# Attention and a gated MLP on one core: another order of the same tasks, and other engines for some of them

## The chip, the cores and the metric

The kernel runs on one core of one Trainium2 chip. The metric is the device time of one execution in microseconds; the median of three runs before the change is 718.39 us (718.02 to 721.24).

## The reference

Eight batches, eight heads, 576 positions, head size 64, model width 512. The reference computes, for every batch and head, scores with a bias that depends on the two positions through a small network, a softmax, and the product with v; the eight heads of a position are then put side by side, and the result goes through a convolution of five taps with a sigmoid (the gate) and two projections.

```python
scores = scale * q @ k.T
x = log1p(abs(i - j)) / log1p(max(i, 1))
bias = relu(x * w1 + b1) @ w2              # one value per head, i and j
attn = softmax(scores + bias)
x = attn @ v                               # heads side by side: 8 x 576 x 512
gate = sigmoid(sum(conv_w[k] * xp[:, k:k+576] for k in range(5)))
out = (gate * (x @ w_val)) @ w_out
```

## The kernel before, in words

The whole work is cut into 3338 tasks, each a function that issues a few instructions on one engine or one DMA. A task lists the tasks it depends on, the engines that may run it with a cost for each, and the buffers it takes and uses. In this version nothing is scheduled when the program is built: two tables, `ORDER` (line 49) and `WHERE`, say in which order the tasks are issued and on which engine each stands (V is DVE, A is ACT, G is POOL, P is TensorE, S is the DMA queue of SP). `Plan.order` walks through the tables, checks that what a task depends on stands before it, and hands out buffers: a ring is a first-in, first-out list of slots, and a slot goes back to the list when the last user of its buffer has been listed. The order of the tables therefore fixes three things: the order of the instructions on each engine, the order of the DMAs in SP's queue, and which earlier tile each buffer is taken over from. Every engine works its list strictly in order.

The stages, with the names and lines that the prediction uses:

- The bias table, 36 strips of 16 positions. Per strip four relu tasks (L450 on ACT, L452 on DVE or POOL), one matmul task (L478), one eviction (L492 on ACT, L494 on DVE), one store to a table in DRAM (L503). Eight strips make one block of 128 rows, of which each bias load (L528, for the last 64 rows L532) reads two heads; a load depends on all stores of its block.
- Attention, 32 pairs of heads, each in five row blocks. Per block: the scores (L929, L949), on DVE the sum with the bias and the row maximum (L800), on ACT the exponential with the row sum (L813, L819), on DVE the reciprocal (L822), on POOL the normalisation (L826), on DVE a transposition in 32x32 blocks (L973, L975). The first six pairs transpose on TensorE instead (L858 to L891) and evict with ACT or DVE (L360, L362). When all five blocks of a pair are turned, TensorE multiplies with v in three tasks of 96 short matmuls each (L1030; the AV tasks), and the result is scaled out of PSUM (L368, L370).
- The weights of the two projections arrive as 64-bit numbers, which DVE and POOL take apart in some ten steps per piece (L548 to L582, L373, L707, L364).
- The MLP, per batch: the convolution (first tap L1095 or L1097; products L1103 on ACT or L1105 on POOL, added up by L1108 on POOL; one of four channel groups adds on DVE with L1093), the sigmoid (L1125), the splitting of x into two halves of 16 bits (L360, L362, L364, then the rest L373), the first projection (L1170), the gate (L1180), the splitting of the gated values, the second projection (L1233), the scaling out of PSUM (L368, L370) and the store.

PSUM holds four tiles for all matmul tasks together (`sp=4`), so a score task can start only when an earlier tile has been read out. Biggest shares of the work are fixed to an engine: L800 and the transpositions to DVE, L813 to ACT, L826 and L1108 to POOL. Free to move are evictions, scalings, splits, the products L1103/L1105 and the relus.

Of the kernel before, what the change touches and what calls it, by code (L numbers as in the profile page):

```python
# [49 lines left out]
    21, 22, 24, 23, 25, 14, 17, 606, 0, 16, 15, 35, 18, 1, 2, 38, 26, 37, 7, 3, 4, 36, 379, 261, 39, 9, 8, 10, 28,  # L50
    29, 11, 42, 44, 377, 30, 31, 5, 32, 257, 119, 40, 121, 378, 375, 45, 267, 268, 122, 120, 258, 43, 123, 56, 33,
    46, 49, 253, 58, 19, 255, 256, 254, 59, 57, 60, 124, 27, 50, 41, 51, 12, 263, 52, 53, 63, 259, 20, 65, 64, 66,
    67, 70, 385, 91, 262, 264, 34, 47, 73, 72, 71, 74, 92, 54, 84, 6, 94, 93, 95, 86, 87, 85, 68, 88, 265, 48, 77,
    61, 78, 125, 80, 266, 386, 79, 98, 99, 376, 100, 81, 112, 427, 89, 105, 101, 82, 115, 113, 13, 384, 114, 96,
    102, 55, 126, 260, 269, 108, 116, 106, 127, 128, 107, 109, 129, 133, 117, 136, 62, 130, 134, 75, 83, 97, 140,
    380, 110, 135, 137, 381, 143, 141, 154, 103, 155, 466, 156, 142, 161, 157, 144, 90, 138, 163, 382, 463, 118,
    162, 76, 147, 149, 148, 150, 158, 104, 131, 145, 164, 165, 69, 168, 170, 151, 166, 171, 159, 182, 111, 184, 183,
    169, 172, 185, 139, 175, 186, 177, 176, 178, 189, 179, 191, 152, 190, 203, 192, 173, 206, 205, 196, 193, 132,
    146, 204, 198, 210, 194, 197, 160, 187, 211, 167, 199, 207, 208, 200, 212, 213, 388, 180, 398, 231, 232, 217,
    219, 153, 174, 214, 218, 201, 234, 233, 465, 220, 215, 224, 226, 225, 221, 467, 469, 470, 195, 188, 476, 475,  # L60
    468, 486, 222, 245, 246, 471, 477, 227, 228, 202, 479, 235, 238, 240, 181, 209, 485, 223, 247, 229, 216, 478,
# [12 lines left out]
    589, 588, 676, 871, 794, 872, 550, 304, 1172, 636, 874, 680, 590, 305, 561, 591, 575, 664, 875, 607, 552, 873,
    554, 659, 306, 307, 662, 576, 665, 663, 876, 656, 658, 657, 660, 308, 309, 310, 528, 877, 880, 661, 560, 311,
    312, 881, 882, 883, 562, 315, 553, 889, 313, 666, 564, 667, 884, 563, 668, 878, 885, 314, 879, 890, 555, 556,
    671, 886, 888, 565, 566, 907, 1176, 675, 567, 568, 569, 316, 672, 887, 892, 317, 677, 557, 577, 669, 908, 673,
    891, 909, 1001, 796, 595, 597, 596, 910, 912, 798, 913, 893, 914, 911, 682, 898, 899, 901, 1034, 678, 559, 799,
    600, 800, 558, 592, 318, 802, 601, 902, 593, 319, 594, 598, 599, 320, 808, 836, 809, 900, 321, 903, 904, 529,
    803, 602, 1023, 842, 811, 837, 322, 817, 323, 843, 945, 894, 838, 844, 327, 906, 905, 918, 810, 895, 812, 919,  # L80
    929, 845, 801, 324, 325, 813, 896, 818, 603, 804, 326, 604, 814, 920, 805, 897, 921, 806, 820, 605, 328, 815,
    693, 922, 979, 826, 827, 915, 934, 329, 829, 944, 684, 946, 819, 807, 821, 847, 816, 822, 823, 916, 850, 948,
    685, 830, 846, 679, 330, 824, 674, 917, 828, 848, 849, 933, 797, 831, 686, 853, 839, 840, 967, 935, 956, 985,
    852, 949, 854, 947, 955, 1012, 832, 834, 937, 938, 936, 841, 331, 950, 939, 332, 863, 977, 833, 957, 959, 851,
    333, 858, 1177, 869, 864, 334, 825, 861, 859, 951, 953, 862, 855, 335, 336, 337, 860, 923, 857, 681, 940, 966,
# [1259 lines left out]
```

## Time and profile before

| | |
|---|---|
| runs | 721.24, 718.39, 718.02 us |
| profiled execution, first to last instruction | 718.7 us, 27193 instructions |
| busy TensorE, DVE, ACT, POOL | 639.9, 604.3, 539.0, 527.9 us |
| mean granted TensorE clock | 0.980 |
| DMA | 140.85 MB, 196 GB/s over the span |

The profiled execution took 718.7 us, 0.3 us more than the median of the runs. Busy time says how long an engine had an instruction in work; TensorE's is the largest, but its matmuls overlap at their ends, and its share is not the same in all stages. So the first look is at a table by stage, the second at what an engine waited for within a stage.

### The profile page before, as it was taken

The page shows a single profiled execution, that of the slowest core. Times are in us where ns is not written, and L with a number is a line of the kernel's source. Part 1 is how long each engine was busy: PE and PEld are TensorE (multiplying, and loading weights), DVE is VectorE, ACT ScalarE, POOL GpSimd, SP SyncE. Part 2 cuts the span into 40 slices and gives each one's busy share as a digit, 9 for nine tenths or more (in the row PEclk, how much of TensorE's full clock was granted, in tenths as well). Part 3 has the DMA queues.
Part 4 walks back from the last instruction along what each step waited for, and adds up shares of the span by engine and source line. Part 5 has one row for each costly group of instructions (what it writes and reads, how often), then busy time and mean ns, then how long its engine had stood idle before and what let it go on. Part 6 is the DMA issues. An engine that isn't in the chain of part 4 may idle for free. (4 is left out here: it accounts for less than half of the span.)

```text
span 718.7 us, 27193 instructions
## 1 busy us (share of the span) xinstructions
PE 639.9 (89%) x11342; PEld 418.8 (58%) x11342; DVE 604.3 (84%) x1341; ACT 539.0 (75%) x1250; POOL 527.9 (73%) x624
## 2 busy tenths in 40 slices
PE   5789698898778989889997999998999999999897
PEld 4455455554456575656464655754765767466653
DVE  6898688889999988888988797798999998888822
ACT  6999688878869747887784797497778875888451
POOL 3633466767978697897888676697878889989852
PEclk9999999999889999999999999998999999999999
DMA  7999877396556655287446564795376555754003
GB/s 275 314 313 319 288 232 251 128 270 211 172 163 205 211 154 194 76 280 253 141 156 213 164 207 140 230 284 189 114 233 247 188 172 143 258 180 133 4 20 114
DMA packets 57355, 140.85 MB, mean 196 GB/s; under 512 B 6160, under 2 KB 7184, under 8 KB 57232
## 3 DMA queue, kind: packets, MB, share of 16 engines
q1 hardware_dynamic: 51984, 129.68, 55.4%
q10 hardware_dynamic: 5248, 9.44, 3.7%
q8 instruction: 89, 1.46, 0.8%
q14 instruction: 34, 0.28, 0.1%
HBM read 118.76 MB, written 20.33 MB: 194 GB/s over the span
## 5 line engine op out<-in xcount | busy, mean ns | idle before, releaser
L826 POOL TENSOR_SCALAR t_d<-t_d,rinv 128x576 f32<-128x576 f32 x256 | 201.4, 797 | 92.2 <-DVE rinv L822 85.3
L813 ACT ACTIVATE t_d<-t_d,nm 128x576 f32<-128x576 f32 x256 | 196.0, 767 | 42.2 <-DVE nm L800 37.5
L800 DVE CUSTOM_DVE_ANT_0 t_d<-t_sp,bias 128x576 f32<-128x576 f32 x256 | 184.7, 746 | 32.6 <-PE t_sp L929 25.2
L929 PE MATMUL t_sp<-t_qk 64*128 64x288 f32 x1024 | 163.8, 438 | 23.6 <-DVE nm L800 11.5
L1030 PE MATMUL t_sp<-t_pt,t_vx 32*64 32x160 f32 (+1 forms) x7488 | 152.2, 298 | 21.6 <-issue 16.1
L1030 PEld LDWEIGHTS t_sp<-t_pt,t_vx 32*64 32x64 f32 x7488 | 131.9, 133 | 46.3 <-issue 32.9
L1108 POOL TENSOR_TENSOR t_w<-t_w 128x576 f32<-128x576 f32 x96 | 138.7, 1448 | 7.6 <-ACT t_w L1103 4.9
L973 DVE STREAM_TRANSPOSE t_pt<-t_d 128x1152 f32<-128x1152 f32 x104 | 140.8, 1362 | 3.3 <-POOL t_d L826 1.8
L929 PEld LDWEIGHTS t_sp<-t_qk 64*128 64x128 f32 x1024 | 93.1, 191 | 73.7 <-issue 19.6
L1170 PEld LDWEIGHTS <-wv 128*128 128x128 f16 x768 | 73.2, 99 | 34.7 <-issue 13.9
L1170 PE MATMUL t_sp<-xh,wv 128*128 128x256 f16 (+1 forms) x512 | 77.1, 291 | 0.5 <-DVE t_w L1180 0.4
L368 ACT ACTIVATE xp<-t_sp,xsc 128x256 f32<-128x256 f32 (+1 forms) x100 | 35.8, 396 | 45.3 <-PE t_sp L1030 43.1
L1233 PE MATMUL t_sp<-wo,gh 128*128 128x512 f16 x256 | 63.1, 380 | 2.0 <-DVE t_w L370 1.0
L1103 ACT ACTIVATE t_w<-xp,convb 128x576 f32<-128x576 f32 x77 | 58.3, 767 | 8.7 <-DMA out<-t_w 4.6
L478 PE MATMUL t_sp<-rel,w 128*32 128x296 f32 (+44 forms) x864 | 49.7, 349 | 12.0 <-ACT rel L450 5.3
L1180 DVE SCALAR_TENSOR_TENSOR t_w<-t_sp,wrel,t_w 128x320 f32<-128x320 f32 (+1 forms) x64 | 31.5, 507 | 24.8 <-PE t_sp L1170 18.6
L452 POOL TENSOR_SCALAR rel<-gt,sct,nb 128x384 f32<-128x384 f32 (+10 forms) x14 | 28.4, 2029 | 32.0 <-PE t_sp L478 13.7
L450 ACT ACTIVATE rel<-gt,b1t,sct 128x496 f32<-128x496 f32 (+17 forms) x74 | 49.5, 745 | 0.7 <-PE t_sp L478 0.7
L478 PEld LDWEIGHTS t_sp<-rel,w 128*32 128x32 f32 x864 | 30.8, 114 | 31.1 <-ACT rel L450 12.1
L813 ACT ACTIVATION_READ_ACCUMULATOR t_d<-t_d,nm 128x1 f32 x256 | 48.2, 188 | 0.0
L819 ACT ACTIVATE rinv<-sm,epst 128x2 f32<-128x2 f32 (+1 forms) x160 | 43.8, 289 | 4.5 <-DVE rinv L822 2.3
L1233 PEld LDWEIGHTS <-gh 128*128 128x128 f16 x256 | 23.1, 98 | 34.6 <-issue 8.6
(127 smaller groups left out, 924.8 us busy)
## 6 DMA issues: line engine op xcount, KB each, us to landing
bias<-bias_d SPq DMA_DIRECT2D x72, 576.0 KB, 6.5
t_vx<-vr SPq DMA_DIRECT2D x78, 384.0 KB, 4.4
t_qk<-qkd SPq DMA_DIRECT2D x32, 576.0 KB, 5.4
bias_d<-t_be SPq DMA_DIRECT2D x36, 295.5 KB, 5.4
t_vx<-vf SPq DMA_DIRECT2D x24, 384.0 KB, 5.0
out<-t_w ACTq DMA_DIRECT2D x32, 256.0 KB, 3.7
biasr<-bias_d SPq DMA_DIRECT2D x36, 144.0 KB, 6.7
t_vx<-vt SPq DMA_DIRECT2D x6, 384.0 KB, 6.8
```

Of the source, the lines that this page charges most:

```text
L450: A.activation(out=rel[g].t[:, 0:w], in_=src, func=AF.Relu, bias=b1t, scale=sct[:, mm : mm + 1])
L478: T.matmul(pb.t[32 * g : 32 * g + 32, x // SPLIT, x % SPLIT : x % SPLIT + y - x], lhsT=w28, rhs=r[:, ::-1] if y <= mid else r, start=True, ...
L800: V.tensor_tensor_reduce(out=eb.t[:, a * S : (a + 1) * S].rearrange("p (j f) -> p j f", j=2), in0=sps[a].t[:, :, 0:HS], in1=bias.rearrange ...
L813: A.activation(out=x, in_=x, func=AF.Exp, bias=st["nm"][:, a : a + 1], scale=-1.0, accum_out=st["sm"][:, a : a + 1])
L826: (G if e == "G" else V).tensor_scalar(out=t, in0=t, scalar1=st["r"][:, a : a + 1], scalar2=1.0, op0=ALU.mult, op1=ALU.mult)
L929: T.matmul(ts[a][:, j, 0:HS], lhsT=qk.t[r, c * P : (c + 1) * P], rhs=qk.t[r, S + j * HS : S + (j + 1) * HS], start=True, stop=True,)
L973: V.transpose(out=x[:, c : 9 - c : 8 - 2 * c, :], in_=eb.t.rearrange("p (a f) -> p a f", a=2))
L1030: T.matmul(avs[i // 2].t[o, i % 2, 0 : 32 * k], lhsT=vxs[j0 // 6].t[r, j - j0, o], rhs=pv[r, 0:k, j, :] if a == 0 else pv[r, 8 : 8 - k : - ...
L1103: A.activation(out=tmp.t, in_=x, func=AF.Copy, scale=cw)
L1108: (V if e == "V" else G).tensor_tensor(out=gates[k].t, in0=gates[k].t, in1=tmp.t, op=ALU.add)
L1170: T.matmul(pm.t[:, d % 2, 0:w], lhsT=pools["wv"][wi][:, k, d * P : (d + 1) * P], rhs=xb.t[xi][:, k, 0:w], start=(q == 0 and k == 0), stop= ...
L1233: T.matmul(pm.t[:, y, :], lhsT=gb.t[gi][:, k, o : o + P] if o < 256 else gx.t[gi][:, k, :], rhs=pools["wo"][wi][:, k, :], start=(q == 0 an ...
```

## The change

Only the two tables change, `ORDER` and `WHERE`. All 3338 tasks are kept, each with its instructions; TensorE and SP keep the tasks they had. The order was searched in a plan that follows the engines event by event in time. A task stands on average 19 places from where it stood, at most 592, and 248 tasks stand on another engine:

| task | from ACT | from DVE | from POOL |
|---|---|---|---|
| product of a tap (L1103, L1105) | 21 to POOL | | 10 to ACT |
| relu | 6 to DVE, 2 to POOL | 2 to ACT, 6 to POOL | 1 to ACT, 2 to DVE |
| first half of x (L360, L362, L364) | 12 to POOL, 12 to DVE | 3 to ACT | 10 to ACT, 3 to DVE |
| rest of x (L373) | | 14 to POOL | 8 to DVE |
| first half of gated values | 9 to POOL, 6 to DVE | 5 to POOL | 12 to ACT, 7 to DVE |
| rest of gated values (L373) | | 8 to POOL | 7 to DVE |
| scaling of the output (L368, L370) | 3 to DVE | 11 to ACT | |
| scaling of AV | 7 to DVE | 6 to ACT | |
| eviction of turned blocks (L360, L362) | 9 to DVE | 11 to ACT | |
| first tap of the convolution | 5 to DVE | 6 to ACT | |
| steps of the weights, bias evictions | 5 to DVE | 3 to ACT, 9 to POOL | 4 to DVE, 3 to ACT |

```diff
 ORDER = (
-    21, 22, 24, 23, 25, 14, 17, 606, 0, 16, 15, 35, 18, 1, 2, 38, 26, 37, 7, 3, 4, 36, 379, 261, 39, 9, 8, 10, 28,
...
+    21, 384, 263, 14, 24, 22, 265, 261, 377, 257, 23, 25, 16, 15, 17, 18, 26, 259, 379, 0, 2, 1, 3, 4, 35, 37, 36,
...
 WHERE = (
-    "VAVVPAVSAAVAPAVAVAVGPVSSPAAVVAPAASVGVPSAAAVSVSVVAVVPAAPASVASVVGAPVSVSAASAPVSSGAVPASAVVSVVVVPAAASVVPA"
...
+    "VSSAVASSSSVPVVVPVSSAVAGPAAAAPVAAVVPVGVAGAAPVVVVVVAVVSSSSSASAAGVPVASSAPVVGAPVAAPVVVAPVAAAVVPVVPAGAVS"
...
```

In SP's queue, in the stage of the bias table, this stood before (stores `bias_d<-t_be`, loads `bias<-bias_d`; the last number of `bias_d` is the block, 94 the first and 98 the last; `bias_0_84` is the tile of row block 0):

```order
L503 DMA bias_d_95<-t_be 16x8x591 x4
L503 DMA bias_d_96<-t_be 16x8x591 x5
L528 DMA bias_0_84<-bias_d_94 128x2x576
L528 DMA bias_1_85<-bias_d_95 128x2x576
L503 DMA bias_d_96<-t_be 16x8x591
L503 DMA bias_d_97<-t_be 16x8x591 x3
L528 DMA bias_1_89<-bias_d_95 128x2x576
L528 DMA bias_2_90<-bias_d_96 128x2x576
```

And this stands there now:

```order
L503 DMA bias_d_95<-t_be 16x8x591 x4
L528 DMA bias_0_84<-bias_d_94 128x2x576
L503 DMA bias_d_96<-t_be 16x8x591
L528 DMA bias_1_89<-bias_d_95 128x2x576
L503 DMA bias_d_96<-t_be 16x8x591 x6
L528 DMA bias_1_85<-bias_d_95 128x2x576
L503 DMA bias_d_97<-t_be 16x8x591
L528 DMA bias_2_90<-bias_d_96 128x2x576
```

The loads have moved nearer to the last store of the block they read: a load of block 95 stood twelve DMAs behind its last store and stands three behind it.

On ACT, at the very start (relus, then the first evictions L492 into the store's buffer), before:

```order
L450 ACTIVATE rel<-gt,b1t,sct 128x512
L450 ACTIVATE rel<-gt,b1t,sct 128x480 x2
L450 ACTIVATE rel<-gt,b1t,sct 128x304
L492 ACTIVATE t_be<-t_sp,cadd 128x592
L450 ACTIVATE rel<-gt,b1t,sct 128x304 x2
```

And now:

```order
L450 ACTIVATE rel<-gt,b1t,sct 128x560 x2
L450 ACTIVATE rel<-gt,b1t,sct 128x304
L492 ACTIVATE t_be<-t_sp,cadd 128x592
L450 ACTIVATE rel<-gt,b1t,sct 128x512
L450 ACTIVATE rel<-gt,b1t,sct 128x480
L492 ACTIVATE t_be<-t_sp,cadd 128x592
```

The first eviction on ACT stood behind fourteen relus and stands behind eleven, and the second follows it sooner.

On DVE, around the last transpositions of the kernel (L973, L975; L1180 is the gate of the batch before, L822 the reciprocals for POOL), before:

```order
L973 STREAM_TRANSPOSE t_pt<-t_d 128x2x576
L822 RECIPROCAL rinv<-rinv 128x1
L822 RECIPROCAL rinv<-rinv 128x2
L1180 SCALAR_TENSOR_TENSOR t_w<-t_sp,wrel,t_w 128x320 x3
L822 RECIPROCAL rinv<-rinv 128x2
L973 STREAM_TRANSPOSE t_pt<-t_d 128x2x576
L975 STREAM_TRANSPOSE t_pt<-t_w 128x576
L973 STREAM_TRANSPOSE t_pt<-t_d 128x2x576 x3
L1180 SCALAR_TENSOR_TENSOR t_w<-t_sp,wrel,t_w 128x320
L362 CAST xh<-xp 128x256
```

And now:

```order
L973 STREAM_TRANSPOSE t_pt<-t_d 128x2x576
L373 TENSOR_TENSOR gl<-t_w,gh 128x256
L373 TENSOR_TENSOR gxl<-t_w,gxh 128x64
L1180 SCALAR_TENSOR_TENSOR t_w<-t_sp,wrel,t_w 128x320
L822 RECIPROCAL rinv<-rinv 128x2
L1180 SCALAR_TENSOR_TENSOR t_w<-t_sp,wrel,t_w 128x320
L822 RECIPROCAL rinv<-rinv 128x2
L973 STREAM_TRANSPOSE t_pt<-t_d 128x2x576 x4
L975 STREAM_TRANSPOSE t_pt<-t_w 128x576
L1180 SCALAR_TENSOR_TENSOR t_w<-t_sp,wrel,t_w 128x320
L370 TENSOR_SCALAR xp<-t_sp,xsc_145 128x2x4x32
```

The last five transpositions follow each other directly now, and the scaling of AV for the last pairs (L370) stands on DVE behind them.

## Rows read from the trace of the kernel before

**Rows 1.** The page: span; busy time, share and instructions of each engine.

```profile
span 718.7 us, 27193 instructions
...
PE 639.9 (89%) x11342; PEld 418.8 (58%) x11342; DVE 604.3 (84%) x1341; ACT 539.0 (75%) x1250; POOL 527.9 (73%) x624
```

**Rows 2.** Windows, six stages: busy time and instructions per engine, clock, DMA.

```profile
core 0: us, PE busy (x) PEld busy (x) DVE busy (x) ACT busy (x) POOL busy (x), PEclk, DMA share, GB/s
0.00:20.00 20.00, 11.77 (x176) 8.00 (x176) 12.82 (x30) 14.26 (x21) 7.74 (x8) 1.00 0.76 260
20.00:80.00 60.00, 49.12 (x783) 30.30 (x780) 50.98 (x127) 57.20 (x103) 26.17 (x19) 1.00 0.96 321
80.00:154.00 74.00, 65.61 (x502) 41.61 (x502) 62.12 (x165) 59.13 (x149) 46.15 (x52) 1.00 0.67 218
154.00:243.00 89.00, 73.37 (x984) 47.66 (x980) 84.59 (x182) 70.04 (x174) 73.18 (x82) 0.92 0.66 213
243.00:660.00 417.00, 389.42 (x8097) 259.08 (x8096) 364.93 (x790) 314.18 (x754) 339.94 (x419) 0.98 0.58 189
660.00:718.70 58.70, 50.60 (x813) 32.15 (x811) 28.84 (x52) 24.22 (x55) 34.73 (x47) 0.98 0.12 42
```

**Rows 3.** Waits of TensorE, 243 to 660: total, times, longest.

```profile
PE t_sp L1030 <- issue: 13.0, 11, 3.8
PE t_sp L929 <- DVE nm L800: 3.5, 4, 1.2
```

**Rows 4.** Timeline of TensorE, 296 to 303: start, length, idle before.

```profile
297.68 2.43 PE L1030 MATMUL t_sp<-t_pt,t_vx 32*64 32x160 f32 x128 [1.05 <-issue]
301.40 0.80 PE L1030 MATMUL t_sp<-t_pt,t_vx 32*64 32x160 f32 x32 [1.29 <-issue]
```

**Rows 5.** Lines: busy, mean ns of one | idle before, releasers.

```profile
L450 ACT ACTIVATE rel<-gt,b1t,sct 128x496 f32<-128x496 f32 (+17 forms) x74 | 49.5, 745 | 0.7 <-PE t_sp L478 0.7
...
L373 POOL TENSOR_TENSOR xl<-xp,xh 128x320 f16<-128x320 f32 (+1 forms) x44 | 33.7, 778 | 5.8 <-ACT xh L360 5.7
...
L1093 DVE SCALAR_TENSOR_TENSOR t_w<-xp,convb,t_w 128x576 f32<-128x576 f32 x32 | 32.6, 1020 | 0.9 <-ACT t_w L1097 0.8
...
L452 POOL TENSOR_SCALAR rel<-gt,sct,nb 128x384 f32<-128x384 f32 (+10 forms) x14 | 28.4, 2029 | 32.0 <-PE t_sp L478 13.7 <-DVE t_be L494 5.1 <-DMA gt<-grel 4.9
...
L373 DVE TENSOR_TENSOR xl<-xp,xh 128x256 f16<-128x256 f32 (+1 forms) x20 | 16.1, 811 | 5.2 <-ACT xh L360 5.1
L494 DVE TENSOR_SCALAR t_be<-t_sp,cadd 128x592 f32<-128x592 f32 x18 | 14.8, 827 | 4.6 <-DMA bias_d<-t_be 3.4 <-PE t_sp L478 1.1
L1105 POOL TENSOR_SCALAR t_w<-xp,convb 128x576 f32<-128x576 f32 x19 | 14.7, 775 | 7.8 <-ACT xp L368 4.7 <-issue 1.2 <-DVE t_pt L975 1.1
...
L362 DVE COPY t_pt<-t_sp 128x512 f32<-128x512 f32 (+2 forms) x19 | 11.7, 634 | 1.8 <-ACT t_pt L360 0.9 <-PE t_sp L858 0.7
...
L370 DVE TENSOR_SCALAR t_w<-t_sp,osc 128x512 f32<-128x512 f32 x13 | 9.7, 746 | 4.5 <-PE t_sp L1233 4.3
...
L373 DVE TENSOR_TENSOR da<-da,wv 128x512 f32<-128x512 f32 x1 | 1.1, 1118 | 0.0
```

**Rows 6.** Waits of SP's queue, 8 to 80: total, times, longest.

```profile
SPq L528 <- DMA bias_d<-t_be: 5.6, 3, 2.7
```

**Rows 7.** Timeline of SP, 8 to 40: start and length of a stretch.

```profile
11.02 7.26 SPq L503 DMA_DIRECT2D bias_d<-t_be  x2
```

**Rows 8.** DMA issues: KB each, median us to landing.

```profile
bias_d<-t_be SPq DMA_DIRECT2D x36, 295.5 KB, 5.4
```

**Rows 9.** The line L1093: shortest, median and longest, in ns.

```profile
L1093 DVE SCALAR_TENSOR_TENSOR t_w<-xp,convb,t_w x32: 777/848/1865, 131.2 to 680.5; 128x576 f32<-128x576 f32 x32
```

**Rows 10.** Windows of 20 us, columns as in rows 2.

```profile
180.00:200.00 20.00, 16.32 (x229) 10.28 (x232) 19.40 (x44) 15.04 (x38) 19.76 (x20) 0.83 0.49 168
600.00:620.00 20.00, 18.90 (x384) 12.32 (x382) 16.95 (x45) 14.92 (x38) 19.05 (x26) 1.00 0.41 123
660.00:680.00 20.00, 18.11 (x547) 13.32 (x547) 18.21 (x31) 12.01 (x30) 19.20 (x25) 1.00 0.01 2
```

More of the change, by code (lines that the diff above doesn't have):

```diff
@@ L256 @@
[L256 to L259 removed]
+    "VSSAVASSSSVPVVVPVSSAVAGPAAAAPVAAVVPVGVAGAAPVVVVVVAVVSSSSSASAAGVPVASSAPVVGAPVAAPVVVAPAVAAAVVPVVPAGAVS"
+    "SSVVSSSAVVGAPVVVVAAPAAGGAAPAAVAASSSSSSVGAPAAAPSAGVPSSSAAGAVPVAAAAVVSSPASSGVPVGAVPVVPAAVGVAAPSVVSVAPA"
@@ new lines @@
+    "VVVPSSASAVVVSSSAAPVAAVAAVVAVVSPVSSSAVPAGPAVPAAVAVVVASSGVGAAAPVVAASSPVSSVAPVVPASVAAVPPVVSVSAAPASVVAVG"
+    "PVSAAVAAPVAVAPVGGGPGPVVAVAAVGVGGGAAAPVPVAVAVGGSSPVPVAAVGGAVSSAASVPPPVAGVVVVAAPPVVVVAAAVGVGGAAAPVAVVS"
+    "SSSPVVGVAAVGPVVPASSSAPVAPVGPAAPPSPSAAPPAAAAVVVVVVSVVAAVGGVAVAAASSSSGGPVVAVPPVVAGAVVVVVVVVGGGAAAVGVPA"
+    "AAAAVGVPPPAPAVPAASVSSSSSSVAGGPVAVAPVVGPAAPVAAAPPAVAGVVGGVPVVSSSPVVVAAAPAAGPAGGGPAAAPVVGGVVVGGPVVAAAA"
+    "AGPVVAAAVVGGPVVAVGGAAVVGGSAPPPAVAAVVVVGGGGGPAAPAPPAAAAVVVPVVAAASSPVVPAPAPAVGVPVAAVGGVVVPVVAAAAAVPVGP"
@@ new lines @@
+    "AVVPVVAPAAVGGAAVGGGGPVVSSSSSSSSSSSAAAAAAPVPVAVAVVGPPAVVVAGGAVVGGPAAPAAGVPPAVVAVAPAASSSSPVVVPAAPVPAGG"
+    "PVSSVSPVAAAVVVPASGGGAGVGVAAAAGGPVVPPSSSSPPVVVVVVGGAAAVAGGAAVGAAAAVVVGAAAGGGVPVVAAAPPAVVGPVVVAAAAPVGV"
+    "AVAPVGGSSAGVVGGVAAAAVGVGGVPSSPVVAAAASVVVVAVVVGGPPAAVAPVVVPVGGAGVVAGGVPVSSSSPVVVAGGGAAVGGVGAAVAVGVVVA"
+    "AAVGGGGPVVVAAAGVPPPAAAVVGGGAAAGGPVVAPVAAVAPVVSPGPGPPPPPPPPVGGVAASVGGAVAAVVVGAAGGVAGVVPPVAAPVGGAAAVAG"
+    "VAAGSSSSSSSPVVPGAAVAAVAVVPVSVVVVAAAVVPPGGPPPPGPVVGGPSSSPSSVVVPGGAAAAVAVAAAAAPPPPPGVVGGPVPPVPPVVGAGVV"
@@ new lines @@
+    "VAAAAAAAVVAAAAAPPVVVPVVGGGGVGAVVSSSPSSSGVPVVVAAVGVGGGGPPPVAAVSPAPAAAAPPPGGGGVGGVAVAVAAAVGVPVVGGGGAGG"
+    "PAAVVAVSSVVPPAAAPVVSPAAGGGGVPVVPPGGGAAVVPPAAVPVVPPPVPPPGGGVGPAAGVVPPVPVVVVGGGVGGGAAAAAAVVSSPSSSPVSSV"
+    "VSSAPSAAAVPVVAAAAAVVVPAAAAGPGGVGGGGVVGGAGPVVPVPVGVPPVPVAAGAAVAVGGGGPSSPVVAAVAAAPAAAAAVGGGVVVVGGAPSSP"
+    "VPVAVAAAPGGGGGVVVVVPPPPPPPPGAGAAAGVGGAGPVAVPPPVAVAAAGGGAVAAGGVVSSPSSSSSVPSSVVAGGGGGGVAAAAPPVAAPVVAAS"
+    "VAAPPVGVAAAGAPVPVVVGGVGPPVVGGVPPVVVAVGGGGPPPAAPSSSSSPVVAAAVVPPAAAAAAPGPVVGPAPVGGAAAGGGPPVVGGGPSVVAAV"
@@ new lines @@
+    "PPPPVPAAVAGPVPVGVAVAAAGGAGGAAGVVPVAVGVVPPPVVVAAAAPASSPVVVVGGPPGGPGPAGGAVVGGGGPAAAGGAAAAVVVVAVVGGVPPP"
+    "PVVAAAAPPVPVPVVAAPPVVGVAAAVVSSSSSSSSSSPPAAAAGGGVVVVVPVAGVVPAGGGGGAAAVVAAPPPPVGPVGVPPVVVSSSPVVSSSSPAA"
+    "AAAAGGGGGGVVPVVAAGAGAAVGGGPVPVVVSAAAGGGPAAAVVVAAGPPGVVPPAVAAAAAPVAAVVVPPAVVGPGGVVAVPPPAPVVPPPPPPPPPG"
+    "GGGVVVPAVVVVVAAAVVGVVGVPPAPVAAAGGASSSPAAAAAAAAVGGGPPVGVVVVVVAAAPPVAVGGGSSGGGGGVGGPAAAPVVVAAPPPPPAAAA"
+    "SSPPPPSPVVVVVAVVVVAAAVGGVPPVVSSSPPGGGGVGGGGGGAAAAVPVVAAGGPPPPVVAAGGPPVAAGAAGVVVPSPAAASSPVAVPVVVAAAAA"
@@ L260 @@
+    "VVVVVPVGGPAVAVAAAVVVVGGGGAAAGAPPPVVVAPPPVGVPPPPPVPPAAAVPPPPVVGGAGGAPVAAPVAVGGVPPPAVVVAAAVVVPPPPPAPVP"
+    "PPVPAAAVGVGPPPVVGPPVVVPPPPPAAPVAAPPPAA"
 )
```

43 lines of the change are left out of this document (10 added, 33 removed), and 346 rows, old and new, of the table ORDER.

## The prediction, made before the changed kernel ran

> **What bounds the kernel now.** I read the shares of the engines first. TensorE is busy for 639.9 of 718.7 us, DVE for 604.3, POOL for 73% of the span [rows 1]. That would say that TensorE bounds it and that an order can give back at most some 79 us. But a share is a mean over stages, so the second view is the table of windows [rows 2], and there the engine that is never idle changes four times. From 20 to 80 us ACT is busy for 57.20 of 60 us and the DMA engines for 0.96 of the time: the bias table is made and moved. From 80 to 154 nothing is full. From 154 to 243 DVE has 84.59 of 89 us (95%). From 243 to 660 TensorE has 389.42 of 417 (93%), DVE 88%, POOL 82%. After 660 TensorE has 50.60 of 58.7, and the other engines run dry. The third view is what TensorE waited for in the long stage: of its 27.6 idle us there, 13.0 stand under "issue", in eleven pieces, all inside runs of AV matmuls; the next is DVE's reading of scores with 3.5 [rows 3]. The timeline shows the form of those eleven: TensorE stops after exactly 128 matmuls, and again after the next 128 [rows 4]. Nothing in the program is waited for there, so a plan that knows only tasks and buffers cannot aim at it; it can only hit it by chance.
>
> **The change, part by part.** No instruction is added or removed, so the sum consists of idle time given back or made. Along TensorE's own order the change is small: a given block of scores has the same work ahead of it within 3 us, added up over all pairs. What moves is the work of the other three, and I count, ahead of the instructions that the path waits for, which tasks stand there less or more, times the mean of their row. All is set against the profiled execution's 718.7 us, 0.3 us above the median of the runs.
>
> Head, to 80 us. The first eviction on ACT stands behind eleven relus, not fourteen: 3 x 745 ns = 2.2 us earlier [rows 5]. A store waits for it at the front of SP's queue, which stood in a stretch of 7.26 us for two stores [rows 7] while the DMA engines were at 0.76 [rows 2], so these 2.2 us count. Over the whole stage ACT gives up five relus (3.7 us), POOL takes them at 2029 ns each, 10.1 us, and has the room (26.17 of 60 busy). But the DMA engines leave only 4% of 60 us, 2.4 us, so more than that can't follow. Against it: the bias loads stand nearer to the stores that they wait for. A store lands 5.4 us after its issue [rows 8]; at 321 GB/s its 295.5 KB take 0.92 us, so a load that stands n DMAs behind the last store of its block waits about 5.4 - 0.92 n. For the eight big loads n was 4, 17, 7, 12, 5, 12, 3, 8, which gives 5.1 us; the row says 5.6 in three waits [rows 6], so the sum holds. Now n is 5, 12, 3, 10, 3, 5, 3, 6, which gives 9.4. SP stands still for 4.3 us more, and all stores behind it. While it stands, three or more transfers are still under way, so most of this is covered; I take a quarter, 1.1, and keep 0 and 4.3 as ends. Head: 1.1 us less, between 4.6 less (2.2 + 2.4) and 2.1 more (4.3 - 2.2).
>
> 154 to 243 us. Ahead of the last scores of this stage DVE has two subtractions of the weights fewer (2 x 1118 ns) and two evictions fewer (2 x 634), one bias eviction more (827) [rows 5]: 2.24 + 1.27 - 0.83 = 2.7 us. Single steps of under a microsecond stand on both sides and I leave them out. DVE is the full engine, so I count all of it: 2.7 less. Below are 0, if DVE only waits instead, and above are the 2.7 with its 4.4 us of idle time.
>
> 243 to 660 us. Ahead of DVE's last transposition stand, beyond those, seven output scalings fewer (746 ns) and eight rests of x fewer (811), and ten first halves and three gated halves more, for which I take 300 ns (no row here; the nearest is the 634 of a copy of 512 columns, and these have about half): 5.2 + 6.5 - 3.9 = 7.8 us. ACT has fourteen products fewer there. So the two engines that free PSUM for TensorE are about 2% lighter in a stage where DVE is 88% busy. What TensorE lost to them is 27.6 - 13.0 = 14.6 us in pieces of about one microsecond. These are handovers that don't go away because a queue is 2% shorter, but a search over all orders can place them better; between nothing and all 14.6 I take a third, 4.9.
>
> The stops under "issue". Of the 78 AV tasks, 24 stood directly behind another AV task, and 19 do now; the rest have scores, projections or evictions' matmuls between. Since the stops come inside such runs, 5/24 of 13.0 us goes: 2.7. If the stops depend on something else (what the DMA engines do at that moment), nothing goes.
>
> Tail. TensorE's order has two pieces of the output projection moved ahead of the last AV task, but its sum from 660 us on is the same, and the drain after the last matmul (scaling, store) too. DVE and POOL stay in turn there, the last five transpositions stand together. I take 0.
>
> Sum: 1.1 + 2.7 + 4.9 + 2.7 = 11.4 us less than 718.7, 707.3 in the profile, 707 for the median.
>
> **What POOL pays.** Ahead of POOL's last normalisation stand 12 products (775 ns), 5 relus (2029) and 8 rests of x (778) more, 25.7 us, and small pieces fewer; about 23 us more work by then. POOL is the emptiest engine (73%), so on the mean this hides in its idle time. DVE's convolution step L1093 reads two tiles from SBUF, and its length goes from 777 to 1865 ns, median 848, mean 1020 [rows 5, 9]: something holds it up at times. The Trainium skill, "SBUF — State Buffer", section "Who interferes with whom", says that a DVE instruction with two SBUF inputs and a POOL instruction that reads SBUF exclude each other, and whichever comes second waits for the whole of the first. This speaks against filling POOL. The spread in the row agrees with it. By that rule 23 us more on POOL would meet such DVE work (L1093 with 32.6 and L373 with 16.1 us are 7% of the span), and 23 x 0.07 = 1.6 us would be added, which makes 709 of the 707; without the rule it stays at 707.
>
> **The rivals.** *No change.* The waits only change their place: TensorE's order is nearly the same, its share of 93% in the long stage leaves little, and DVE's 2.7 us can turn into waiting for scores. Against it speaks that DVE, ACT and POOL are all better filled where they were short. Time: 718, between 715 and 722.
>
> *Slower, by POOL.* In three stretches of 20 us POOL has no room: 19.76, 19.05 and 19.20 us busy [rows 10], 2.0 us free together. The last shows it best: between the normalisation that ends near 660 us and the last one POOL's queue held 10.6 us of work (row means added in its order) and holds 13.8. Every normalisation is waited for by a transposition, and an AV task waits for all five. If each of the three stretches gets 3.2 us more, 9.6 - 2.0 = 7.6 us pass to the end. One of the three lies in DVE's stage, so its 2.7 us are lost too, and those of TensorE with them; the head's 1.1 stays. Time: 718.4 + 7.6 - 1.1 = 725. It decides as soon as POOL's work between two normalisations is longer than the stretch has time; that DVE got lighter doesn't help then.
>
> *Much faster.* All of the 14.6 us of TensorE's handovers go, DVE's stage gives 7.1 and the head 4.6, no stop does: 718.4 - 26.3 = 692.
>
> **How the numbers follow.** A difference of 0.5% (3.6 us) is about what a measurement of this kernel can tell from none. The forecast of 707 (own range 698 to 714) has 0.52, much faster 0.12, no change 0.15, slower 0.21, in which I also count a head that gets dry behind the loads. Faster by over 0.5% is 0.64, within it 0.15, slower 0.21. The range goes from 690, just below "much faster", to 725, which holds half of the POOL case; about 0.11 lies above and some 0.06 below, and the rest up to 0.2 is for what I didn't think of.
>
> **What would show it.** In the profile after: the window from 20 to 80 us with ACT below 57 and the first scores of the second pair earlier by 1 to 3 us, SP's waits for stores near 9 us instead of 5.6; DVE's stage shorter by about 3 us; TensorE idle for 20 us or less in a window of the long stage of the same work, with the stops under "issue" near 10 us; POOL about 550 us busy. I would be wrong if the normalisations start later behind POOL's own queue and DVE's transpositions wait for them, or if the stops under "issue" grow.

## The result, and the profile after

The kernel before and the changed kernel were timed in turn on one chip, and later once more beside the experiments:

| runs | before, median us | changed, median us | changed / before, 95% interval |
|---|---|---|---|
| first series, 6 and 6 | 718.20 (715.17 to 721.24) | 724.17 (720.38 to 727.04) | 1.0108 [1.0068, 1.0149] |
| beside the experiments, 35 and 12 | 717.24 (709.55 to 724.31) | 720.16 (714.01 to 727.17) | 1.0046 [1.0005, 1.0088] |

So the change made the kernel slower, by 3 to 6 us. The forecast was 707, 11 us faster; both medians lie in its range of 690 to 725, but its sign was wrong. The two series differ for one and the same changed kernel by 4.0 us in the median (724.17 and 720.16; for the kernel before by 1.0), so a difference of 3 or 4 us between two medians below is at the edge of what these runs can tell. The ratios leave disturbed runs out; since single runs of these kernels lie up to 11 us from their median, that also cuts some of their own upper runs, and so the medians of all runs stand beside the ratios here and below.

The page of the changed kernel, 723.58 us in its profiled execution, answers to [rows 1]:

```profile
span 721.8 us, 27165 instructions
...
PE 645.1 (89%) x11342; PEld 419.1 (58%) x11342; DVE 604.5 (84%) x1347; ACT 533.0 (74%) x1231; POOL 545.4 (76%) x637
```

POOL has 17.5 us more and ACT 6.0 less, as the table of engines says. The windows, columns as in [rows 2]:

```profile
0.00:20.00 20.00, 10.69 (x175) 7.66 (x178) 13.45 (x30) 13.26 (x18) 9.25 (x9) 1.00 0.82 289
20.00:80.00 60.00, 49.24 (x769) 29.87 (x762) 52.58 (x124) 52.99 (x91) 31.43 (x21) 0.94 0.92 301
80.00:154.00 74.00, 66.22 (x515) 41.30 (x511) 65.04 (x169) 63.70 (x160) 53.70 (x59) 1.00 0.67 224
154.00:243.00 89.00, 76.08 (x984) 49.23 (x983) 79.91 (x173) 69.00 (x172) 74.23 (x83) 0.87 0.59 190
243.00:660.00 417.00, 387.49 (x8075) 256.69 (x8074) 352.51 (x777) 307.51 (x738) 339.97 (x425) 0.99 0.60 194
660.00:721.80 61.80, 55.38 (x841) 34.31 (x838) 40.97 (x79) 26.58 (x56) 36.83 (x45) 1.00 0.12 40
```

Much of this looks as forecast: ACT fell from 57.20 to 52.99 in the head, and DVE from 84.59 to 79.91 behind 154 us. But from 243 to 660 DVE did 12.4 us less than before [rows 2], and that work stands behind 660 (40.97 for 28.84): work is late there, not gone. What TensorE waited for in that stage answers to [rows 3]:

```profile
PE t_sp L1030 <- issue: 12.0, 12, 2.7
PE t_sp L949 <- DMA t_qk<-qkd: 5.8, 3, 2.6
PE t_sp L929 <- DVE nm L800: 2.6, 4, 0.9
```

The second row is new: three waits for a load of q and k from HBM. The same stage, cut where the loss turned out to lie (243 to 264 and 500 to 600), in the changed kernel:

```profile
243.00:264.00 21.00, 17.44 (x437) 12.94 (x437) 13.67 (x36) 12.96 (x33) 12.84 (x15) 1.00 0.64 207
264.00:500.00 236.00, 220.20 (x4504) 142.85 (x4491) 207.09 (x446) 179.05 (x424) 197.56 (x244) 1.00 0.61 199
500.00:600.00 100.00, 92.56 (x1927) 62.50 (x1926) 81.84 (x178) 69.58 (x171) 76.54 (x102) 0.95 0.50 160
```

and in a second profile of the kernel before (the run e16 below):

```profile
243.00:264.00 21.00, 20.37 (x460) 14.43 (x456) 18.86 (x42) 15.49 (x40) 15.59 (x21) 1.00 0.42 132
264.00:500.00 236.00, 217.07 (x4362) 141.66 (x4360) 203.27 (x440) 176.05 (x418) 190.91 (x230) 0.99 0.60 199
500.00:600.00 100.00, 98.08 (x2176) 67.44 (x2176) 94.85 (x202) 79.21 (x193) 84.44 (x111) 1.00 0.58 193
```

In the first and the last of these stretches all engines do less in the changed kernel, in the middle one all do more. At the start of the first stands this, on SP (start, length of the stretch of issues):

```profile
225.34 0.33 SPq L779 DMA_DIRECT2D t_qk<-qkd  x1
226.10 3.33 SPq L528 DMA_DIRECT2D bias<-bias_d  x3
...
241.00 0.35 SPq L779 DMA_DIRECT2D t_qk<-qkd  x1
```

and on TensorE:

```profile
249.31 1.20 PE L949 MATMUL t_sp<-t_qk 64*64 64x288 f32 x16 [2.60 <-DMA t_qk<-qkd]
```

The second q/k load is issued at 241.00 and takes 8.3 us to where TensorE goes on. In the kernel before the same load went out 14.6 us earlier:

```profile
226.40 0.54 SPq L779 DMA_DIRECT2D t_qk<-qkd  x1
```

Its buffer seems free at 228.1 in the changed kernel, when TensorE's last scores from an earlier load end (225.75 + 2.36):

```profile
225.75 2.36 PE L929 MATMUL t_sp<-t_qk 64*128 64x288 f32 x16 [0.44 <-ACT xp L368]
```

It stands there in SP's queue behind thirteen transfers of bias and values, issued from 226 to 239 us. The planner prices a q/k load at 1.73 us and a bias load at 1.85 (the `("S", 1.85 ...)` in `load_bias`); the page has 5.9 us from issue to landing for the one and 6.7 for the other. The Trainium skill, "DMA: Bandwidth & Descriptors", section "Anatomy of one DMA — SWDGE (gpsimd) path", prices one transfer that GpSimd issues at 2.0 us and its bytes at 436 GB/s; worked out for 576 KB that is an estimate of 3.4 us for a load alone. The loads here are issued by SP; the shortest q/k load of the changed kernel took 3.5 us, the median 5.9 and the longest 10.4, so the estimate fits the shortest alone.

### The profile page after: what moved, and what is told of

The parts are those of the page before. It is cut to its first block, busy times and chain, and to the rows that moved or that the text cites. A ratio compares the mean times of both kernels' runs of the same rounds, so it can differ in the third digit from the quotient of the medians.

```text
span 721.8 us, 27165 instructions
## 1 busy us (share of the span) xinstructions
PE 645.1 (89%) x11342; PEld 419.1 (58%) x11342; DVE 604.5 (84%) x1347; ACT 533.0 (74%) x1231; POOL 545.4 (76%) x637
## 5 line engine op out<-in xcount | busy, mean ns | idle before, releaser
L929 PE MATMUL t_sp<-t_qk 64*128 64x288 f32 x1024 | 164.6, 440 | 22.9 <-DVE nm L800 12.9
L1030 PE MATMUL t_sp<-t_pt,t_vx 32*64 32x160 f32 (+1 forms) x7488 | 156.4, 301 | 17.7 <-issue 12.0
L1030 PEld LDWEIGHTS t_sp<-t_pt,t_vx 32*64 32x64 f32 x7488 | 134.3, 135 | 45.2 <-issue 30.3
L973 DVE STREAM_TRANSPOSE t_pt<-t_d 128x1152 f32<-128x1152 f32 x104 | 141.4, 1366 | 6.5 <-POOL t_d L826 5.3
L929 PEld LDWEIGHTS t_sp<-t_qk 64*128 64x128 f32 x1024 | 92.9, 191 | 76.0 <-issue 21.2
L1233 PE MATMUL t_sp<-wo,gh 128*128 128x512 f16 x256 | 64.9, 380 | 2.1 <-ACT gh L360 1.3
L478 PE MATMUL t_sp<-rel,w 128*32 128x296 f32 (+40 forms) x864 | 50.4, 358 | 14.5 <-DVE t_be L494 4.2
L452 POOL TENSOR_SCALAR rel<-gt,sct,nb 128x304 f32<-128x304 f32 (+13 forms) x19 | 37.3, 1966 | 34.3 <-PE t_sp L478 16.6
L368 ACT ACTIVATE xp<-t_sp,xsc 128x256 f32<-128x256 f32 (+1 forms) x98 | 35.4, 397 | 36.5 <-PE t_sp L1030 34.7
L1103 ACT ACTIVATE t_w<-xp,convb 128x576 f32<-128x576 f32 x66 | 50.0, 766 | 13.6 <-DVE t_w L1180 5.1
L373 POOL TENSOR_TENSOR gl<-t_w,gh 128x256 f16<-128x256 f32 x51 | 35.3, 694 | 16.3 <-DVE gxh L362 9.5
L1180 DVE SCALAR_TENSOR_TENSOR t_w<-t_sp,wrel,t_w 128x320 f32<-128x320 f32 (+1 forms) x64 | 31.3, 507 | 18.9 <-PE t_sp L1170 13.3
L450 ACT ACTIVATE rel<-gt,b1t,sct 128x496 f32<-128x496 f32 (+15 forms) x69 | 46.2, 743 | 0.9 <-PE t_sp L478 0.8
```

What stands on the lines that cost most here:

```text
L450: A.activation(out=rel[g].t[:, 0:w], in_=src, func=AF.Relu, bias=b1t, scale=sct[:, mm : mm + 1])
L478: T.matmul(pb.t[32 * g : 32 * g + 32, x // SPLIT, x % SPLIT : x % SPLIT + y - x], lhsT=w28, rhs=r[:, ::-1] if y <= mid else r, start=True, ...
L929: T.matmul(ts[a][:, j, 0:HS], lhsT=qk.t[r, c * P : (c + 1) * P], rhs=qk.t[r, S + j * HS : S + (j + 1) * HS], start=True, stop=True,)
L973: V.transpose(out=x[:, c : 9 - c : 8 - 2 * c, :], in_=eb.t.rearrange("p (a f) -> p a f", a=2))
L1030: T.matmul(avs[i // 2].t[o, i % 2, 0 : 32 * k], lhsT=vxs[j0 // 6].t[r, j - j0, o], rhs=pv[r, 0:k, j, :] if a == 0 else pv[r, 8 : 8 - k : - ...
L1103: A.activation(out=tmp.t, in_=x, func=AF.Copy, scale=cw)
```

## The experiments

All but e16, a single execution, were timed in turn with the kernel before. The theories: POOL (the forecast's rival: normalisations late behind POOL's own work, called QUEUE where one place is meant), STRETCH (one stretch behind 488 us loses), LOADS or QK (loads issued too late), SUM (many small waits). In e1 to e4 the tables take 40 more lines of the file, so that L969 there is L929 elsewhere. The edits are shown in short form: in each kernel it is the contents of the two tables that differ.

**Engines alone, order alone.**

```diff
 # e1: order of before, engines of the changed plan; e2: the other way round
-for n, e in zip(ORDER, WHERE):
+for n, e in zip(ORDER_BEFORE, WHERE_AFTER):
```

> The order of before (all engines and the SP queue), with the 248 changes of engine that the changed plan makes. Theory POOL (normalisations come late behind the products and splits that moved to POOL's queue): the loss is in the engines alone, so about 724 us, POOL busy near 545. Theory STRETCH (the loss lies in the order of one stretch, 500 to 640 us, where loads and buffers come late): about 718, no loss. A gain to about 714 would say that the engines are the good part of the change.

> The order of the changed plan, with every task on the engine that it had before. Theory POOL: about 718, since POOL's queue is again the old one. Theory STRETCH: about 724 or more, with the loss again between 500 and 640 us.

Measured: e1 745.44 us, ratio 1.0404 [1.0363, 1.0446]; e2 786.29, ratio 1.0964 [1.0910, 1.1019]. Both theories miss. Engines and order fit only each other: each half of the change is far worse than the whole, so nothing can be said of "the engines" or "the order" alone.

**Cuts.** The first tasks of the two orders, up to any place, are nearly the same set (at most 17 differ), so one plan can be continued with the other.

```diff
 # e3: cut where the changed kernel stood at 488 us; e4: the other way, at 508 us
-ORDER = after
+ORDER = after[:2296] + [t for t in before if t not in after[:2296]]
```

> The changed plan up to the point that it reaches at 488 us, the plan of before for everything behind it (order and engines). Theory STRETCH, in the form that the changed plan's own tail is bad: the lead of 3 to 7 us of work that the changed kernel has at 480 to 500 us stays, about 713. In the form that a lead can't be kept there, whatever the tail, since loads and stores end it: about 718, with PE idle between 500 and 640 well above the 3.7 us of before. Theory POOL: in between, about 721, for 158 of the 248 changes of engine are still in it.

> The plan of before up to the point that it reaches at 508 us, the changed plan behind it. Theory STRETCH with a bad tail: 718 and the 11 to 13 us that the changed kernel loses between 500 and 640, less what it wins behind 640: 726 to 730. With a lead that can't be kept: about 719, since there is no lead to lose. Theory POOL: about 720 (87 of the 248 changes of engine).

Measured: e3 713.34 us, ratio 0.9950 [0.9921, 0.9979], before 717.75; e4 724.88, ratio 1.0129 [1.0082, 1.0176]. The bad tail is seen from both sides: the same first part with the other tail is 7 to 11 us faster, and the tail on the other first part costs 7, in which a cost of the seam itself can be hidden (e13 below has one).

e8 moves the cut, e11 puts the changed plan into the middle alone, e13 to the front alone, and e12 is the changed kernel itself:

> The changed plan up to the point that it reaches at 568 us (it reached 488 in the run that gave 713), the plan of before behind it. If the whole loss falls before 568 (places such as 518, 541 and 551 to 559), the lead is gone here too: 720 to 722. If it falls behind 568, the lead is kept: 713. Theory SUM, with the loss spread evenly over 488 to 640: half of it, about 717 to 719.

> The plan of before up to the point that it reaches at 264 us, then the changed plan up to the point that it reaches at 488 us, then the plan of before: 68 of the 248 changes of engine. The traces say that the changed plan is 4 us of work behind at 260 and 5 us ahead at 488 to 500. If these add, and the lead is kept as in the run that gave 713: 708 to 711. If the changed plan's gain in its middle only makes up what its start lost (its buffers are then drained differently), 713 to 718.

> The changed kernel as it is, beside the others on the same chip, as their yardstick: 722 to 726 by every theory.

> The changed plan up to the point that it reaches at 264 us, the plan of before behind it (88 of the 248 changes of engine). The forecast's terms for this stretch (head 1.1, DVE stage 2.7) say 713 to 714. The profiled execution of the changed kernel, which is 3.8 us of TensorE's work behind at 260, says 721. The difference between two runs (the changed plan to 488 less the changed plan from 264 to 488, 4.75 and 2.2 us faster) says 714 to 715.

Measured: e12 720.16, as in the first table. e8 720.23 us, ratio 1.0053 [1.0027, 1.0078], as if the whole loss fell before 568 us; but its trace loses 6.4 us from 560 to 580, where its seam lies, and no other kernel loses more than 4.9 there, so part of this can be the seam's; e11 713.81 (before 717.24), ratio 1.0000 [0.9961, 1.0039], about the level of e3; e13 725.14, ratio 1.0121 [1.0064, 1.0179], slower than any expectation. Its trace loses 5 us between 264 and 300, behind the seam, where neither plan alone does. A cut can itself cost that much, and e13 says nothing about the front.

**Single places in the tail.** Two theories had a place each. At 518 us a product that the change put on POOL waits for a buffer whose output is still being stored, and three normalisations stand behind it (POOL, then the DVE transposition that needs the first):

```profile
517.76 0.67 POOL L373 TENSOR_TENSOR xl<-xp,xh 128x256 f16<-128x256 f32 x1
521.02 0.75 POOL L1105 TENSOR_SCALAR t_w<-xp,convb 128x576 f32<-128x576 f32 x1 [2.59 <-DMA out<-t_w]
521.74 0.75 POOL L826 TENSOR_SCALAR t_w<-t_w,rinv 128x576 f32<-128x576 f32 x1
```

```profile
522.52 0.78 DVE L975 STREAM_TRANSPOSE t_pt<-t_w 128x576 f32<-128x576 f32 x1 [3.05 <-POOL t_w L826]
```

```diff
 # e5, POOL's queue
-product, norm, norm, norm
+norm, norm, norm, product
 # e6, SP's queue; e7: both
-narrow bias, 2 values, bias, values, q/k, 3 bias
+2 values, bias, values, q/k, 3 bias, narrow bias
```

> The changed kernel with one of its 3338 tasks moved: the product on POOL that waits 2.59 us for an output store at 518 to 521 us is queued behind the three normalisations that followed it, no buffer changes. Theory QUEUE (normalisations late behind other work in POOL's queue start the loss): DVE's wait of 3.05 us and TensorE's stop of 2.69 us at that place are gone, and the time is 2 to 5 us shorter, 719 to 722. Theory SUM (the loss is made of many small waits in the stretch behind 488 us, none of which decides): no change that can be measured, 723 to 725.

> The changed kernel with one load moved in SP's queue: the load of the narrow bias that waits 18.6 us for its old reader at 515 to 533 us is issued behind the eight loads that followed it. Theory LOADS (loads stand too long in SP's queue, then land together, and a q/k load lands 8.3 us after its issue): the DMA share of 540 to 560 falls from 0.86 towards the 0.59 of before, TensorE's wait of 2.50 us for that load at 559 is gone, 2 to 5 us shorter, 719 to 722. Theory SUM: 723 to 725. Theory QUEUE: no change.

> The two moves of the runs before together. If both theories hold, the gains add, 716 to 720; if one, as that run; theory SUM: 723 to 725.

Measured: e5 719.05 us, ratio 0.9999 [0.9963, 1.0036]; e6 723.17, ratio 1.0101 [1.0061, 1.0141]; e7 727.10, ratio 1.0140 [1.0094, 1.0187]. e5's trace does what was expected for POOL and DVE (the product's wait is 0.20 us, DVE's is gone). TensorE's stop at the place is not the product's doing: it is 1.32 us in e5, and it was 1.59 in e12, where the product waits 2.64; it is one of the stops under "issue", on which more below. In e6's trace TensorE's wait for the q/k load has grown from 2.50 to 4.91 us. But e7 contains the same move and is not faster than e6. So e6's load is no cause, and whether e5's move is worth anything is not settled.

What all kernels with this tail share, and no other, is a wait at 550 to 559 us. In the changed kernel, on the chain of waits (start, length, what) and on TensorE:

```profile
550.39 8.33 DMA t_qk<-qkd
```

```profile
558.85 2.20 PE L949 MATMUL t_sp<-t_qk 64*64 64x288 f32 x16 [2.50 <-DMA t_qk<-qkd]
```

The load goes out as soon as its buffer is free, but behind bias loads that are not needed for 24 us and more, and in the window behind it DVE, ACT and POOL are short and the clock is down:

```profile
560.00:580.00 20.00, 20.00 (x522) 16.08 (x521) 15.33 (x32) 13.38 (x31) 12.15 (x17) 0.87 0.38 118
```

```diff
 # e9, SP's queue; e10: and POOL's as in e5; e14: e4 with this move
-bias(579 us), bias, bias, values, bias(574 us), q/k
+bias, bias, values, q/k, bias(574 us), bias(579 us)
```

> The changed kernel with two bias loads (needed at 574 and 579 us) moved in SP's queue from in front of the q/k load of 550 us to behind it; nothing else moves. Theory QK (the loss of 540 to 580 us begins with TensorE's wait for that q/k load, which takes 8.3 us beside the bias loads that are in flight, and the clock falls behind the wait): the load lands in about 5 us, TensorE's wait of 2.5 us is gone, the granted clock of 560 to 580 is 1.0 in place of 0.87, and the time is 3 to 5 us shorter, 719 to 721. Theory SUM: the wait moves to the next late thing, 723 to 725.

> That and the product on POOL behind its three normalisations, as in the run that gave 719. If both causes hold, 714 to 717; if only the product's, 719; if neither, 723 to 725.

> The plan of before up to 508 us and the changed plan behind it (725 us in its run), now with the two bias loads behind the q/k load. Theory QK: 720 to 722, and no wait of TensorE for that load. Theory SUM: 724 to 726.

> The changed kernel with both moves (the product behind the normalisations, the bias loads behind the q/k load) up to the point that the changed kernel reaches at 600 us, the plan of before behind it. If what is left of the loss behind 488 us lies behind 600: 712 to 714. If it lies between 488 and 600 in places that the moves don't mend: 716 to 717.

Measured: e9 716.55 us, ratio 1.0001 [0.9960, 1.0043]; e10 718.16, ratio 0.9992 [0.9938, 1.0045]; beside them the changed kernel had 720.16. e14 722.01, ratio 1.0092 [1.0056, 1.0129], for e4's 724.88. e15 719.92, ratio 1.0060 [1.0018, 1.0102]. In e9 TensorE no longer waits for the load, and the window behind is full again:

```profile
547.32 1.20 PE L949 MATMUL t_sp<-t_qk 64*64 64x288 f32 x16 [0.18 <-ACT t_w L368]
```

```profile
560.00:580.00 20.00, 19.27 (x373) 12.21 (x372) 17.78 (x40) 17.60 (x41) 16.52 (x23) 1.00 0.50 165
```

The mechanism is shown: with the bias loads behind it the q/k load came in time. Its price is not clear of noise: about 3 us in two pairs of runs (720.16 to 716.55 beside each other, 724.88 to 722.01 from two series), but 0.9 in a third (e5's 719.05 to e10's 718.16), and e17 below, which has the move too, is level with e12. e15 misses: with the old tail from 600 on it is not faster than e10.

**All late loads.** From eighteen profiles (the two kernels, e3 to e18) I worked out how much earlier (+) or later (-) than in the first profile of before the same amount of work was done, summed over the four engines, each task counted at the length that it has in that first profile. The change of this lead over a stretch, mean and ends over the kernels that have the stretch whole from one plan (those that mend the stretch left out, except where said):

```
stretch    plan of before            changed plan               difference
0-80       -3.3 (5: -6.2 to  0.0)    -3.4 (13: -5.5 to -1.8)     -0.2
80-154      0.0 (5: -1.7 to  2.6)    +3.9 (13: +3.2 to +4.8)     +3.9
154-243    -0.9 (5: -1.8 to  0.3)    +0.4 (13: -1.8 to +2.4)     +1.2
243-264    +0.3 (5:  0.0 to  0.7)    -4.9 (11: -7.2 to -2.8)     -5.1
264-500    +4.9 (4: -0.1 to  8.6)   +10.1 (10: +8.8 to +11.2)    +5.2
500-600    +1.4 (6: -0.1 to  2.1)    -8.9 (changed, e12)        -10.2
600-end    +0.4 (6: -0.3 to  1.1)    +2.9 (10: +2.6 to +3.1)     +2.5
```

The differences sum to -2.7, a loss of 2.7 us, near what was measured. Two stretches lose 15.3, the others gain 12.6. The gain of 5.2 in 264 to 500 lies within the spread of the four profiles of before there (-0.1 to 8.6); the loss in 243 to 264 and the one in 500 to 600 lie outside theirs. From 580 to 600 the loss is at a bias load; in the changed kernel's chain:

```profile
585.40 6.43 DMA bias<-bias_d
```

It is issued at 585.40, 23 us later than in before, behind loads that wait for TensorE, and DVE's next scores start at 592.00, behind it (DVE itself is idle 0.58 us for it, and 0.96 for a load of values before it). e17 mends all three places by loads alone:

```diff
 # SP's queue; e18: only the first of these, in e3
-8 loads, q/k(241 us)                   two bias loads, q/k(550 us)     values ..., bias(585 us)
+q/k(241 us), 8 loads                   q/k(550 us), two bias loads     bias(585 us), values ...
```

> The changed kernel with five loads moved in SP's queue and nothing else (same instructions on the same engines in the same order, same buffers): the q/k load that was issued at 241 us in front of nine loads, at about 229; two bias loads behind the q/k load of 550 us, as in e9; two bias loads, of which one was issued at 585 us, to about 562. Theory LOADS (the planner prices a load at 1.7 to 1.9 us and puts it as late as that allows, the chip takes 5 to 8 us to land it): the three stretches cost the changed kernel 4.6, 4.5 and 2.3 us of lead on the mean of the profiles; without them 722 becomes 710 to 713. If only the second is real, 717 to 719, as e9. If the loss is elsewhere: 722.

> The changed plan up to 488 us and the plan of before behind it (713 us in its run), with the q/k load of 241 us issued at about 229. Theory LOADS: the loss of 4.6 us between 243 and 264 is gone, 708 to 711. Otherwise 713 to 714.

Measured: e17 719.70 us, ratio 1.0074 [1.0031, 1.0116]; e18 713.30, before 716.74, ratio 0.9991 [0.9944, 1.0038]. So LOADS in its strong form falls. In e17's trace the waits at two of the places are gone. Its lead changes by -1.9 in 560 to 580 (-0.9 in e9, e10 and e14; -4.9 to -0.8, on the mean -3.4, in the six with this tail that don't mend it), which alone would not tell it from those six, and by +0.1 in 580 to 600 (nine others: -2.4 to -1.1). But 243 to 264 still costs it 7.1. The q/k load went out at 230.37 there, and TensorE no longer waits for it, but DVE waits for a bias load, and TensorE stops at the same place all the same:

```profile
248.19 0.76 DVE L800 CUSTOM_DVE_ANT_0 t_d<-t_sp,bias 128x576 f32<-128x576 f32 x1 [4.36 <-DMA bias<-bias_d]
```

```profile
249.73 1.20 PE L949 MATMUL t_sp<-t_qk 64*64 64x288 f32 x16 [2.25 <-issue]
```

This wait of DVE is not new. It stands at the same place where nothing was moved, in e12:

```profile
247.95 0.76 DVE L800 CUSTOM_DVE_ANT_0 t_d<-t_sp,bias 128x576 f32<-128x576 f32 x1 [4.57 <-DMA bias<-bias_d]
```

and, with 1.73 to 5.05 us, in every other profile with this part of the plan but the changed kernel's first, where DVE's wait of 2.87 us is put down to TensorE. So two loads were late here, the q/k load and this bias load, and e17 and e18 moved only the one; the account above, by the q/k load alone, was half of it. In 225 to 239 us this plan issues fourteen transfers. The Trainium skill, "DMA: Bandwidth & Descriptors", section "Queues, rings and completion order", says that each DMA engine takes the descriptors of a ring in their order; e9 and e17 agree with it in so far as the load moved to the front came in time. And 520 to 540 costs e17 4.6; POOL's product still waits in front there, but whether that is the reason e5 and e7 leave open.

**How far a single profile goes.**

> The kernel before once more, for a second profile of the same instructions. By every theory 712 to 721; open is by how much its windows differ from the first profile's: if by less than 2 us up to 260 us, the stage by stage comparison of single profiles stands, if by more, it doesn't.

Measured: 717.43 us. Its windows to 243 us, columns as in [rows 2]:

```profile
20.00:80.00 60.00, 48.38 (x755) 29.48 (x748) 47.87 (x118) 53.87 (x94) 24.13 (x16) 0.96 0.95 315
80.00:154.00 74.00, 67.79 (x507) 42.52 (x507) 62.48 (x166) 60.42 (x152) 45.67 (x53) 0.96 0.64 212
154.00:243.00 89.00, 74.22 (x983) 48.50 (x981) 83.96 (x179) 68.40 (x169) 73.18 (x82) 0.88 0.63 208
```

The same instructions are 3.9 us behind the first profile at 243 us, and 9.3 behind in e11, which has them too. ACT's 57.20 of 60 us in [rows 2], from which the forecast called ACT full, is 53.87 here. Only what repeats over several profiles can be read by stage.

## Why the prediction was wrong

**The step that failed** is what was left out of the sum. The prediction says: "What moves is the work of the other three", and it follows SP's queue only in the head. Behind 80 us no load was followed, though the order shows them moved: the q/k load of 226 us behind thirteen other transfers, to 241, the bias load of 562 to 585. The two stretches that cost 5.1 and 10.2 us have no term in it. Three of the waits in them, at 249, 559 and 592 us, are for loads, which the traces show at the same place in every kernel that has that part of the plan unmended. The wait at 559 is worth 1 to 4 us by the runs with and without it, that at 592 about 2 by e17's trace. The one at 249 could not be mended by moving the q/k load, since a bias load of the same burst was as late. That these waits make up the whole loss is not shown: e17, without two of them, is as slow as e12.

**Head, 1.1.** Not there: -3.4 against -3.3 at 80 us. ACT is below 57 as forecast, but so it is in before's second profile, and the first row was an unusual execution. SP's waits for stores came to 4.0 us, not to the 9 that the estimate from the order gave. The clock is 0.94 in 20 to 80 where before had 1.00 and 0.96.

**DVE stage, 2.7.** In 154 to 243 the gain is 1.2. The larger one, +3.9 between 80 and 154, where thirteen profiles all lie between +3.2 and +4.8, has no term in the sum.

**Handovers 4.9 and stops 2.7.** Gains of 5.2 in 264 to 500, and of 2.5 behind 600 (where 0 was forecast for the tail), stand against 7.6. But the third taken of the handovers was a choice, and 5.2 is no larger than the spread of before's own profiles, so the near agreement shows nothing of the mechanism. TensorE's idle time in the long stage was to be 20 us or less and is 29.5. The stops under "issue" in the long stage are 12.0 in the changed kernel and 10.0 in e12, for 13.0 and 11.6 in before's two profiles: on the mean 1.3 of the 2.7 us. The prediction put them down to AV tasks behind each other and said that nothing in the program is waited for. The traces show what ends them: the arrival of a packet of instructions. The kernel moves 89 packets of 16 KB on a queue that the profile calls "instruction":

```profile
q8 instruction: 89, 1.46, 0.8%
```

That is one packet in 8 us; TensorE's 22684 matmuls and weight loads make 255 for each, and stops that follow each other are 128 matmuls, each with its weight load, apart [rows 4]. In two profiles of each kernel 40 of the 42 stops of 0.2 us and more in this stage end 1.0 to 1.6 us after the end of such a packet. No run tested whether fewer AV tasks behind each other make them shorter.

**POOL.** The rival's time, 725, is what the first series gave, but the rival is not shown by that. POOL has 17.5 us more work [rows 1], and the prediction's own sign of being wrong, transpositions that wait for normalisations, did appear. In the changed kernel:

```profile
DVE t_pt L973 <- POOL t_d L826: 5.3, 11, 1.4
...
DVE t_pt L975 <- POOL t_w L826: 3.1, 1, 3.1
```

and in before:

```profile
DVE t_pt L973 <- POOL t_d L826: 1.8, 3, 0.9
```

The wait of 3.1 us is the product that waits for a store, which is the price of a buffer and not of POOL's work. The other eleven are 3.5 us more than before's three; whether they cost time was not tested (e9 and e10 have 6.5 and 6.4 us of them and are 4 and 2 us faster than e12). DVE's convolution step, which would have met POOL more often, has a median of 820 ns for 848 [rows 9], and 822 in before's second profile. So of the 1.6 us that the prediction worked out from the rule in the Trainium skill, "SBUF — State Buffer", section "Who interferes with whom", this row shows nothing.

**Open.** What the rest of the loss behind 488 us is. e9 and e10 are level with before and e3 is 3 us faster than they: their tail still costs something that one profile each, with spans of 707.9 and 706.4 us well below their medians, doesn't show. A mend of the burst at 225 us that also brings the late bias load to the front, or sends its two bias loads that are not needed before 276 us later, wasn't tried. The best version is e3, the changed plan to 488 us and the old one behind it: 713.34, 0.5% faster than before; e18, the same but for one load, has 713.30 with an interval that includes no change.

## What to carry to other kernels

When a plan moves transfers, list for each load its issue and first use before and after, and set the difference against the time to landing in the trace, not against the plan's price; a load in a burst pays for all those in front of it. Before one late load is moved, see who else waits at that place: here a second load of the same burst was as late, and moving the first gave nothing. To find where a searched plan loses, continue one plan with the other at a cut and compare from both sides; a cut whose seam loses by itself, as e13's, tells nothing. And take a second profile before a stage's numbers are used: here two of the same instructions differed by 4 us by stage, as much as the terms of the sum.

## What the runs showed of the hardware

The granted clock of the same instructions differs from run to run (1.00 is 2.4 GHz throughout; what lies below is a mean with stretches at 1.2 GHz): in 80 to 154 us it was 1.00 and 0.96 in the two profiles of before and 0.90 in e11. And a load of 576 KB has no one price: median 5.4 us for q/k and 6.5 for bias in before, and in 538 to 560 us of the changed kernel, where 6.29 MB move at 286 GB/s, bias loads have a median of 8.6:

```profile
bias<-bias_d SPq DMA_DIRECT2D x4, 576.0 KB, 8.6
```

And an engine can wait for its own instructions: TensorE's stops of 0.2 to 3.8 us in runs of short matmuls end 1.0 to 1.6 us after a packet of 16 KB on the queue "instruction" has come, 10.0 to 13.0 us in all from 243 to 660.
